# A delta-rule block and a multiplicative FFN: scaling U on ScalarE, head by head, under a new list of steps

## The chip, the cores and the metric

The kernel runs on one core of a Trainium2 chip. The metric is the time of one launch in device microseconds, as the median of the runs. "PE" is TensorE (PEld its weight loads), "DVE" VectorE, "ACT" ScalarE, "POOL" GpSimd and "SP" SyncE, which issues all transfers here.

## The reference

A delta-rule attention over 4 batches x 8 heads x 768 tokens x 48 features, and behind it a feed-forward block whose two branches are multiplied.

```python
k_n = k / (np.linalg.norm(k, axis=-1, keepdims=True) + 1e-06)
for t in range(S):
    y[:, :, t] = np.einsum('bhd,bhde->bhe', q[:, :, t], state)
    v_old = np.einsum('bhde,bhd->bhe', state, kt)
    state = state + bt[:, :, :, None] * np.einsum('bhd,bhe->bhde', kt, vt - v_old)
...
a = x @ w1
b = x @ w2
h = a * b @ w3
return (h @ w_out).astype(np.float32)
```

x is y with the heads side by side: 3072 tokens x 384. The weights come as 64-bit floats and are converted on the chip. w3 and w_out are multiplied into one matrix first (384 wide), and the products of the feed-forward block use a scheme with sums of weights and of tokens that needs fewer products.

## The kernel before

The 768 tokens are cut into 12 chunks of 64. For each chunk:

- **scores** (step name `s`): K K^T and K Q^T for 4 batches x 8 heads. It works in two halves (`r` = 0, 1: two of the four batches each). A half is 48 small products into one pair of PSUM banks (a `ps_w` tile, L433 and L439). One part of it, scaled by beta and the key's norm for each token and head (`wt`), is U (L445, written to `U`). The other is copied to `PT` (L457) and masked (L459). There are two such pairs of banks, taken in turn by all the small products: scores, corner, chain and outputs, and by the inverse, which holds one of them.
- **to_blocks** (`u`), **inverse** (`V`), **corner** (`e`): (1 + U) is inverted for two chunks at once. Blocks of 32 x 32 of U are brought into another layout: for the first two pairs of chunks by copies (L492) and a transpose (L508), for the other four pairs by transfers to DRAM and back (`Ud` L499, `Ub` L510). VectorE then takes 31 steps of two operations (L530/L535 or L541/L546). The result goes back in the same way (L589, or `Vd` L559 and `TT` L571), is transposed (`T`, L599), and two small products (L616) make the block off the diagonal.
- **chain** (`c`): three products (L687) with the state of the chunk before and with the inverse, with VectorE in between (L718, L727, L749). This is the recurrence over chunks. **outputs** (`y`) makes y of the chunk (L786), and ScalarE copies it to `xT` (L805).

Around these stand the loads of k, q, v (`k`, `p`, `v`) and of weights (`P`, converted by ScalarE, VectorE and GpSimd: L837, L840, L842, L844), the fold of w3 and w_out (`t` L880, `f` L895), and the feed-forward block: for the first two chunks plain products (`a`, `b`, L915), for each later pair of chunks products with sums (`m`, L1117, four `ps_f` banks), sums of tokens and of slabs (`G`, `S`, both L200) and the output products (`o`, L1199) with their results (`x`).

Every step is a generator. `ORDER` is a table of 1705 names, written out; each name runs its generator to the next `yield`, and this order holds on every engine. An apostrophe gives a step's elementwise work to the other engine: with it, a sum (L200) goes to VectorE in place of GpSimd, and a copy (L204) to ScalarE or VectorE, whichever it was not.

Of the kernel before, what the change touches and what calls it, by code (L numbers as in the profile page):

```python
# [44 lines left out]
P16 k3 g1 V0 P17 V0 f1 f2 f0 f0 f0 f1 V0 V0 P15 P15 V0 s1 zp t5 P16 f1 P19 P15 V0 zp P17 V0 t6 f2
P18 V0 V0 f2 t6 P16 zp zp P16 p2 V0 P18 g1 t9 V0 P23 v0 t7 P18 f3 V0 g1 P19 t8 V0 t8 t7 P19 P19 f3
t9 P18 t10 V0 d2 V0 P22 P23 t10 P29 d2 zp V0 t11 t11 V0 g1 f4 V0 n0 V0 V0 s0 P23 P23 P20 n0 P22 f5
f4 f5 V0 d2 V0 V0 V0 P22 f3 P29 N1 V0 P21 P21 P20 p3 P22 N1 t14 t15 e0 e0 e0 e0 N0 e0 d2 s2 t14 f5
P20 P20 e0 e0 e0 P25 P25 e1 e1 e1 f4 t12 d3 s2 s2 v1 d3 s2 P29 s2 u2 s2 c0 t12' c0 f7 P24 P24 P29 e1
c0 p3 c0 t15' P25 P21 d3 P26 y0 P28 c1 n1 n1 y0 f6 P26 d3 c1 u2 P21 e1 s3 P24 s3 s3 t13 P26 y0 P27  # L50
e1 s3 e1 f7 t13 s3 s3 P24 u2 e1 f7' u3 P26 u3 c1 P25 s1 u3 V1 V1 V1 b3 P28 b3 P27 b2 b2 c1 N1 p4 V1
V1 V1 V1 V1 y1 y1 P31 P27 P27 P28 V1 V1 V1 b0 f6 V1 V1 V1 V1 V1 V1 f6 P31 b0 c1 c1 b1 P30 P30 P28 b7
b5 c2 V1 V1 d4 b1 y1 a04 a04 b7 a05 a05 b5 a01 a02 a00 P31 P31 P32 P34 a03 P33 V1 V1 V1 V1 a01 a02
P34 a06 b6 v2 V1 V1 a03 a00 n2 P30 P35 d4 a06 P32 V1 b4 P34 V1 V1 V1 P33 P32 P33 p4 a07 P30 n2 P32
V1 V1 V1 V1 V1 V1 b6 b4 b1 c2 b1 P35 a07 P34 b3 P35 e2 b3 P33 zp e2 e2 a03 P35 e2 a02 a01 e2 b7 e3 W
e3 e3 e2 e2 W' k5 k4 d4 a03 d4 b5 W' e2 c2 e3 b7 a02 T c2 g2 g2 a01 p5 v3 a00 g2 g2 g2 g2 g2 y2 c2
y2 d5 d5 b4 a06 T b5 W c2 n3 b4 g2 a00 n3 T e3 T a06 N2 N2 a04 a07 b2 p5 s4 W e3 a04 v4 a07 s4 d5 k6
b2 s4 s4 s4 s4 s4 a05 d5 a05 c3 c3 u4 s5 s5 s5 s5 s5 s5 s5 u5 V2 b0 e3 N2 b6 b0 S0' S0' p6 b6 S0 e3
c3 S0 V2 V2 g3 W W' oA0 W' W' c3 S0 W n4 n4 W S0 s5 xA0 g3 S0' c3 oA0 W S0 c3 V2 V2 y3 oD0 xA0 S0 S0
S0 V2 V2 V2 V2 V2 V2 V2 V2 d6 S0 S0 V2 W S0 oB0 oC0 xA0 s4 V2 V2 V2 xB0 V2 y3 y3 V2 V2 V2 oB0 xB0 V2  # L60
c4 xC0 G1 S0 S0 W V2 V2 xD0 V2 d6 V2 xC0 G1 m10 G1 G1 oC0 G1 G1 m10 m10 m10 m10 m10 m10 xC0 G1 G1 W
W W G1 V2 V2 p6 k7 V2 m10 m10 m10 m10 V2 V2 V2 V2 V2 m10 m10 m10 m10 m10 m10 m10 G1 m10 V2 V2 V2 xC0
xD0 m10 m10 m10 m10 e4 d6 W W W m10 m10 m10 m10 m10 m10 m10 m10 m10 m10 m10 m10' m10 m10 G1 d6 m10
m10 m10 m11 e4 e4 m10 g3 e4 G1 m10 m10 m11 m11 m10 m10 m10 c4 g3 g3 g3 g3 g3 e4 e4 m11 p7 m11 c4 m11
c4 m10' y4 e5 d7 d7 m11 N3 p7 v5 n5 m11 m11 N3 m11 m11 m11 m11 y4 m11 m11 s6 m11 m11 m11 s6 s6 m11
m11 m11 v6 s6 n6 s6 e5 m11 e5 s6 d7 s6 d7 m11 m11 m11 e5 s7 s7 s7 s7 s7 s7 s7 u7 u6 V3 m11 m11 m11
m11 m11 n5 m11 m11 c4 e5 m11 m11 c4 c5 c5 m11 m11 m11 S1 m11 m11 e5 V3 m11 c5 m11 m11 m11 oA1 p8 k8
c5 m11 m11 m11 m11 y5 S1 V3 V3 V3 V3 V3 V3 V3 S1 S1 oD1 S1 S1 xA1 y5 y5 oB1 oA1 xA1 V3 V3 V3 V3 V3
V3 V3 S1 xB1 V3 d8 V3 d8 V3 oB1 xB1 xA1 p8 V3 V3 xD1 oC1 V3 V3 xC1 S1 xC1 G2 m20 G2 G2 G2 G2 G2 G2
G2 G2 m20 m20 m20 V3 xD1 m20 m20 n6 V3 V3 m20 m20 V3 oC1 c5 g4 V3 xC1 V3 V3 V3 V3 V3 V3 m20 m20 m20  # L70
N3 xC1 k9 m20 m20 m20 m20 m20 V3 V3 m20 V3 e6 m20 g4 m20 m20 m20 m20 c5 s6 m20 m20 m20 m20 m20 m20
m20 m20 m20 m20 d8 m20 c6 c6 e6 G2 G2 G2 m20 m20 m20 m20 m20 m20 m20 g4 m20 e6 m21 m20 d8 p9 m20 e6
e6 m20 m21 s8 e7 v7 g4 m21 e6 c6 g4 g4 g4 g4 m20 m20 m20 n7 c6 N4 m21 m21 m21 m21 y6 N4 s8 m21 d9 d9
# [30 lines left out]
def kernel(  # L104
# [311 lines left out]
    def by_parity(x):  # L416
        return x.rearrange("p (a e) t -> p a e t", e=2)
# [978 lines left out]
```

## Time and profile before

| | |
|---|---|
| median of 3 runs | 547.52 us (545.92 to 552.04) |
| the profiled execution | 546.43 us, its span 544.7 us |
| TensorE busy | 511.2 us (94%) |
| weight loads busy | 429.7 us (79%) |
| VectorE busy | 406.1 us (75%) |
| GpSimd busy | 274.8 us (50%) |
| ScalarE busy | 220.3 us (40%) |
| transfers, share of 16 engines | 45.9% on the queue that SP issues |

Shares are of the span and are averages over stages: transfers and conversions of weights fill the first 80 us, the products of the feed-forward block everything from about 100 us on. In a group's row the columns are: line, engine, operation, out<-in, shapes, count | busy us, mean ns of one | idle time of the engine just before, and what ended it. In a row of the timeline: start, length, engine, line, operation, count, and in brackets the idle time before it. In the chain of waits: start, length, what. A matmul of 32-bit data leaves two records, so a step of 32 products has 64.

### The profile page before, as it was taken

What the parts mean: (1) busy time and instruction counts of PE and PEld (TensorE: products, weight loads), DVE (VectorE), ACT (ScalarE), POOL (GpSimd) and SP (SyncE); (2) the same over time, 40 slices, a digit from 0 to 9 for tenths busy, and PEclk for the clock granted to TensorE, in tenths of its full rate; (3) what the DMA queues carried; (4) which work ended last, traced back from release to release, by engine and by line L of the source; (5) the groups of instructions that cost most, each with busy time, mean ns of one, the idle gap of its engine ahead of it and who ended that gap; (6) DMA issues with size and microseconds to landing.
All of it is one profiled execution on the core that took longest, in us unless ns stands there. A gap on an engine that the chain in (4) does not pass through costs nothing.

```text
span 544.7 us, 19913 instructions
## 1 busy us (share of the span) xinstructions
PE 511.2 (94%) x8460; PEld 429.7 (79%) x8460; DVE 406.1 (75%) x882; ACT 220.3 (40%) x452; POOL 274.8 (50%) x295
## 2 busy tenths in 40 slices
PE   3599898999999999999999999999899999999997
PEld 2475565788888987889888789878799888997887
DVE  1789985799778988768987789968688766436553
ACT  3696676847423134432236251343421342412210
POOL 4565664416968994157642487443267301240140
PEclk9999999999999999999999999999999999999999
DMA  8978995668565155644446641654402220020001
GB/s 235 256 194 236 222 163 108 133 147 137 81 104 105 30 126 83 97 90 79 80 93 93 112 88 43 130 84 73 99 19 59 64 51 4 14 76 0 2 0 58
DMA packets 197592, 52.64 MB, mean 97 GB/s; under 512 B 184576, under 2 KB 191872, under 8 KB 197504
## 3 DMA queue, kind: packets, MB, share of 16 engines
q1 hardware_dynamic: 197504, 51.38, 45.9%
q8 instruction: 66, 1.08, 0.8%
q14 instruction: 22, 0.18, 0.1%
HBM read 41.25 MB, written 8.91 MB: 92 GB/s over the span
## 4 chain that ended last, share of the span: by engine, by line
PE 79%; DVE 7%; DMA 5%; ACT 3%; issue 2%; SPq 2%; POOL 1%; DVEq 0%; POOLq 0%; ACTq 0%
PE ps_f L1117 32%; PE ps_f L1199 17%; PE ps_f L915 8%; PE ps_w L687 6%; PE ps_w L786 4%; PE ps_w L616 3%; DMA raw<-in_moe_w_dram 3%; PE ps_f L895 2%; PE ps_w L433 2%; PE ps_w L439 2%; DVE ps_w L535 1%; DVE tb L530 1%; DMA ktok<-in_k_dram 1%; PE ps_f L880 1%; DMA perm<-in_q_dram 1%
## 5 line engine op out<-in xcount | busy, mean ns | idle before, releaser
L200 POOL TENSOR_TENSOR ab<-ab 128x512 f32<-128x512 f32 (+1 forms) x57 | 66.7, 1186 | 65.8 <-DVE ab L1148 33.5
L1199 PE MATMUL ps_f<-w,ab 128*128 128x192 f32 x376 | 65.4, 328 | 0.0
L1117 PE MATMUL ps_f<-xT,w2s 128*128 128x256 f32 x240 | 62.3, 390 | 1.1 <-DVE x_room L1148 0.8
L1117 PE MATMUL ps_f<-xT,w1s 128*128 128x256 f32 x240 | 63.1, 387 | 0.0
L1199 PEld LDWEIGHTS ps_f<-w,ab 128*128 128x128 f32 x376 | 61.8, 191 | 0.9 <-DVE osb L1229 0.2
L1148 DVE TENSOR_TENSOR ab<-ab,ps_f 128x512 f32<-128x512 f32 x70 | 47.4, 680 | 19.2 <-PE ps_f L1117 17.6
L1117 PEld LDWEIGHTS ps_f<-xT,w1s 128*128 128x128 f32 x240 | 43.6, 190 | 10.1 <-issue 1.7
L1117 PEld LDWEIGHTS ps_f<-xT,w2s 128*128 128x128 f32 x240 | 43.7, 190 | 9.8 <-DVE x_room L1148 1.4
L1199 PE MATMUL ps_f<-room,ab 128*128 128x192 f32 x272 | 47.0, 329 | 0.3 <-POOL ab L200 0.2
L546 DVE TENSOR_TENSOR ps_w<-ps_w,tb 128x31 f32<-128x31 f32 (+15 forms) x124 | 43.3, 349 | 4.5
L895 PE MATMUL ps_f<-w2s,w3T 128*128 128x384 f32 x128 | 43.9, 491 | 2.1 <-ACT w3T L204 1.2
L541 DVE TENSOR_TENSOR tb<-ps_w,Ub 128x31 f32<-128x31 f32 (+15 forms) x124 | 41.8, 337 | 4.6 <-DMA Ub<-Ud 1.5
L1199 PEld LDWEIGHTS ps_f<-room,ab 128*128 128x128 f32 x272 | 44.2, 190 | 1.2 <-POOL ab L200 0.5
L805 ACT COPY xT<-ps_w 48x256 f32<-48x256 f32 x96 | 30.5, 365 | 30.4 <-PE ps_w L786 29.8
L1117 PE MATMUL ps_f<-xT,room 128*128 128x256 f32 x160 | 40.3, 384 | 0.0
L673 POOL TENSOR_TENSOR vtok<-vtok,n 128x384 f32<-128x384 f32 x24 | 19.7, 830 | 37.8 <-DMA vtok<-in_v_dram 37.8
L200 POOL TENSOR_TENSOR ab<-ab,x_room 128x512 f32<-128x512 f32 x10 | 12.7, 1274 | 50.0 <-DVE x_room L1148 50.0
L895 PEld LDWEIGHTS ps_f<-w2s,w3T 128*128 128x128 f32 x128 | 23.5, 190 | 17.9 <-POOL w2s L844 1.8
L200 POOL TENSOR_TENSOR xT<-xT 128x256 f32<-128x256 f32 x44 | 32.1, 741 | 7.9 <-DVE xT L200 4.6
L1145 ACT COPY x_room<-ps_f 128x512 f32<-128x512 f32 x20 | 11.7, 585 | 59.4 <-PE ps_f L1117 58.5
L459 POOL TENSOR_TENSOR PT<-PT,smask 128x512 f32<-128x512 f32 x20 | 25.9, 1297 | 17.0 <-ACT PT L457 17.0
L1148 DVE TENSOR_TENSOR x_room<-x_room,ps_f 128x512 f32<-128x512 f32 x40 | 27.3, 682 | 9.1 <-PE ps_f L1117 8.1
(192 smaller groups left out, 1080.6 us busy)
## 6 DMA issues: line engine op xcount, KB each, us to landing
raw<-in_moe_w_dram SPq DMA_DIRECT2D x16, 512.0 KB, 5.5
ktok<-in_k_dram SPq DMA_DIRECT2D x48, 96.0 KB, 3.4
vtok<-in_v_dram SPq DMA_DIRECT2D x24, 192.0 KB, 4.3
raw<-in_moe_w_dram SPq DMA_DIRECT2D x24, 192.0 KB, 4.1
out_dram<-osb SPq DMA_DIRECT2D x46, 96.0 KB, 1.7
raw<-in_moe_w_out_dram SPq DMA_DIRECT2D x8, 384.0 KB, 5.0
perm<-in_k_dram SPq DMA_DIRECT2D x40, 64.0 KB, 3.3
perm<-in_q_dram SPq DMA_DIRECT2D x32, 64.0 KB, 2.8
```

The source lines that it names most:

```text
L200: (dve if other else pool).tensor_tensor(out=out, in0=x, in1=y, op=op)
L459: pool.tensor_tensor(out=PT, in0=PT, in1=smask[:].unsqueeze(1).to_broadcast([P, H, C]), op=ALU.mult)
L541: dve.tensor_tensor(out=tv, in0=V[:, 0 : s + 1, s : s + 1].to_broadcast([P, s + 1, n]), in1=U[:, s, s + 1 : BS].unsqueeze(1).to_broadcast( ...
L546: dve.tensor_tensor(out=o, in0=o, in1=tv, op=ALU.subtract)
L687: pe.matmul(out(ps, r, h, z), lhsT=lhs(r, h, z), rhs=rhs(r, h, z), start=True, stop=True,)
L786: i = pe.matmul(region(h, z, r), lhsT=lhs, rhs=rhs, start=part[n] not in part[:n], stop=part[n] not in part[n + 1 :],)
L805: act.copy(out=xT[f, cc, p:NP:2, b : b + NR, :].rearrange("p a r t -> p r a t"), in_=pyv[f, z, b : b + NR],)
L895: pe.matmul(ps[:, 0:DM], lhsT=w3Ts[jc, kc // 4][:, kc % 4 * P : kc % 4 * P + P], rhs=wo[:, kc], start=(i == 0), stop=(i == KF - 1),)
L915: pe.matmul(ps[:].rearrange("p b c t -> p b (c t)"), lhsT=w[:, m, js], rhs=x[:, c0, m], start=(m == 0), stop=(m == KM - 1),)
L1117: pe.matmul(ps[:, n * g : n * g + n].rearrange("p (b c t) -> p b c t", b=HB, c=2), lhsT=product_weights(i, 2 * r + g), rhs=of[i], start=na ...
L1148: dve.tensor_tensor(out=t, in0=t, in1=cell(what[2]), op=op)
L1199: pe.matmul(ps[b][:, b, :], lhsT=block(u, HF * f + i, z)[:, P * b : P * b + P], rhs=ws_[w][:, i], start=first and i == 0 and (b == 0 or n ...
```

## The change

For the chunks 4 to 11, U of a half is no longer made by one VectorE step over 128x512, but by eight ScalarE operations of 128x64, one for each head, each with that head's column of `wt` as its scale. Chunks 0 to 3 stay as they were. All 1705 steps stand in a new list; each name occurs as often as before, but apostrophes have moved: 18 of the slab sums' steps have one in place of 10, 11 of the token sums' in place of 7, 16 of the `m` steps in place of 13.

```diff
-P11 beta P2 P0 P11 P11 P11 P2 beta P3 k0 K0 P0 beta P0 P0 K0' K0 P6 P6 q0 P2 zd P9 P3 Q0 P2 P6 P3 g0
-g0 g0 k1 P8 Q0' P6 P3 g0 Q0' P9 Q0' K0 P9 g0 g0 g0 P9 zp P8 P10 q1 K0' K1 P13 P10 Q0' s0 P12 P10 P8
...
+P11 beta P2 P0 P11 P11 P11 P2 beta P3 k0 K0 P0 beta P0 P0 K0' K0 P6 P6 P3 K0' q0 P2 zd zd P2 g0 g0
+g0 k1 g0 P6 Q0 g0 P3 g0 P6 K0 P5 P5 P5 Q0 K1 K1 Q0' K1 K1 Q0' P10 P9 P3 P5 P10 q1 P12 g0 g0 P9 Q0 N0
...
-            dve.tensor_tensor(
-                out=by_parity(u[:, r]), in0=psv[:, :, :, 0, :],
-                in1=by_parity(
-                    scale_of(ws, m)[:, r].unsqueeze(2)
-                ).to_broadcast([P, NP, 2, C]),
-                op=ALU.mult,
-            )
-            yield
+            if m < 4:
+                dve.tensor_tensor(
+                    out=by_parity(u[:, r]), in0=psv[:, :, :, 0, :],
+                    in1=by_parity(
+                        scale_of(ws, m)[:, r].unsqueeze(2)
+                    ).to_broadcast([P, NP, 2, C]),
+                    op=ALU.mult,
+                )
+                yield
+            else:
+                for h in range(H):
+                    act.mul(
+                        out=u[:, r, h], in_=psv[:, h // 2, h % 2, 0, :],
+                        mul=scale_of(ws, m)[:, r, h : h + 1],
+                    )
+                yield
```

Lines behind the new code stand 8 higher in the changed kernel (L457 is L465, L616 is L624, and so on); the eight operations are its L456.

The first place is ScalarE's queue in the third round of inverses, chunks 6 and 7. Before (L457 is the PT copy of a score half, L641 and L661 the copies of a corner, L516 the start of an inverse, L1141 and L1145 empty banks of the `m` products):

```order
L457 COPY PT<-ps_w 128x512
L1145 COPY ab<-ps_f 128x512
L457 COPY PT<-ps_w 128x512
L641 COPY T_104<-ps_w 32x2x8x32 x2
L457 COPY PT<-ps_w 128x512 x2
L1145 COPY x_room_97<-ps_f 128x512
L661 ACTIVATE TT_94<-ps_w 32x2x8x32 x2
L516 COPY ps_w<-eye 128x1023
```

and now (L456 is U, L465 the PT copy):

```order
L456 ACTIVATE U_103<-ps_w,wt 128x64 x8
L465 COPY PT<-ps_w 128x512
L1153 COPY ab<-ps_f 128x512
L649 COPY T_104<-ps_w 32x2x8x32 x2
L456 ACTIVATE U_103<-ps_w,wt 128x64 x8
L465 COPY PT<-ps_w 128x512
L456 ACTIVATE U_103<-ps_w,wt 128x64 x16
L465 COPY PT<-ps_w 128x512 x2
L669 ACTIVATE TT_94<-ps_w 32x2x8x32 x2
```

Each PT copy has eight operations ahead of it, and in the third group two halves' U stand ahead of both their PT copies: the second half of chunk 7 and the second half of chunk 6, which comes last in the new list (before, chunk 7's did).

The second place is the same round on VectorE. Before (L445 is U, L390 makes K^T and Q^T of a later chunk, L1148 and L1143 belong to the `m` products, L749, L718 and L727 to the chain):

```order
L445 TENSOR_TENSOR U_103<-ps_w,wt 128x512
L390 STREAM_TRANSPOSE KQ<-perm_95 128x8x64 x2
L1148 TENSOR_TENSOR x_room_97<-x_room_97,ps_f 128x512
L445 TENSOR_TENSOR U_103<-ps_w,wt 128x512 x2
L1148 TENSOR_TENSOR ab<-ab,ps_f 128x512 x3
```

and now (L1156 and L1151 are the former L1148 and L1143, L726 the former L718):

```order
L390 STREAM_TRANSPOSE KQ<-perm_95 128x8x64 x2
L726 TENSOR_TENSOR vtok<-vtok,ps_w 128x768
L1156 TENSOR_TENSOR ab<-ab,ps_f 128x512
L1156 TENSOR_TENSOR x_room_97<-x_room_97,ps_f 128x512
L329 TENSOR_REDUCE ss<-sq 128x8
L1156 TENSOR_TENSOR ab<-ab,ps_f 128x512 x3
L200 TENSOR_TENSOR ab<-ab 128x512
L1151 TENSOR_TENSOR ab<-ps_f,ab 128x512
L200 TENSOR_TENSOR ab<-ab 128x512
```

The U steps are gone, and sums of slabs (L200) that GpSimd made stand among the `m` steps.

The third place is ScalarE's queue at the start, ahead of the first inverse. Before (L492 copies blocks of U, L837 and L840 convert a piece of weights):

```order
L492 COPY xT_79<-U_103 32x32x16
L492 COPY xT_79<-U_103 96x32x16
L837 ACTIVATE w2s<-raw 128x384
L840 ACTIVATE raw<-raw 128x384
L492 COPY xT_79<-U_103 32x32x16
L516 COPY ps_w<-eye 128x1023
```

and now (L500 is the former L492, L524 the former L516):

```order
L465 COPY PT<-ps_w 128x512
L500 COPY xT_79<-U_103 96x32x16
L500 COPY xT_79<-U_103 32x32x16
L524 COPY ps_w<-eye 128x1023
L529 COPY ps_w<-eye 128x1
```

The conversion that stood between the last two copies of U has moved away.

More of the change, by code (lines that the diff above doesn't have):

```diff
@@ L45 @@
[L45 to L49, printed above, removed]
@@ new lines @@
+k10 y7 oD2 S2 S2 S2 S2 oB2 V4 m21 V4 V4 V4 V4 V4 V4 V4 V4 xA2 xB2 V4 V4 V4 V4 d10 V4 d10 V4 oC2 S2
+oA2 S2 oB2 xA2 xB2 xC2 c7 xA2 xC2 xD2 S2 G3 G3 G3 m30 V4 V4 V4 V4 V4 oC2 xC2 s8 G3 G3 G3 G3 G3' V4
+V4 p10 m30 m30 m30 m30 m30 m30 m30 m30 m30 m30 m30 V4 G3 G3 n8 G3 G3 m30 m30 m30 V4 V4 V4 m30 m30
+m30 V4 m30 m30 m30 m30 m30 m30 m30 m30 m30 m30 m30 V4 V4 k11 v9 xD2 n9 n8 g5 c7 n9 m30 m30 m30 m30
+c8 xC2 V4 e8 c8 d10 e8 m30 m30 m30 m30 m30 m30 m30 m30 e8 m31 g5 e8 m30 g5 g5 m30 d10 e8 e9 m31 g5
+g5 m30 m30' m30 p11 m31 e8 m31 m31 g5 g5 c8 c8 m30' N5 m31 m31 m31 m31 m31 y8 c8 N5 d11 d11 e9 m31
@@ new lines @@
+m31 c8 p11 m31 m31 m31 m31 m31 y8 e9 e9 s10 s10 s10 m31 m31 m31 s10 s10 m31 m31 d11 c9 s10 s10 c9
+d11 m31 m31 s11 s11 s11 s11 s9 s11 m31 m31 m31 m31 m31 s11 u10 u11 V5 m31 m31' m31 e9 s11 m31 m31
+m31 m31 m31' m31 m31 v11 e9 c9 m31 m31 m31 m31 m31 m31 S3' c9 oA3 xA3 m31 s11 S3 S3 S3 y9 V5 N5 m31
+V5 V5 V5 V5 V5 V5 V5 oD3 v10 S3 n10 oB3 y9 oA3 V5 V5 V5 V5 V5 V5 V5 xB3 S3 S3 S3 xA3 oC3 oB3 y9 V5
+V5 V5 G4 G4' xA3 V5 c9 m40 xB3 xC3 G4 xD3 xC3 n10 G4' G4 G4 G4 G4 G4 G4 V5 V5 V5 oC3 c9 xC3 V5 V5
+m40 m40 m40 m40 m40 m40 m40 m40 m40 n11 G4 m40 m40 m40 m40 m40 V5 V5 V5 V5 V5 c10 m40 m40 m40 m40 V5
@@ L100 @@
+S5' S5 S5' S5 S5' o5 x5 x5 x5 o5 x5 x5 x5 x5 x5 x5 o5 x5 x5 x5 x5
 """
```

98 lines of the change are left out of this document (45 added, 53 removed).

## The prediction

> **What bounds the kernel now.** I read the page first, then the stretches of the span, then the chain and the groups of instructions.
>
> ```profile
> span 544.7 us, 19913 instructions
> PE 511.2 (94%) x8460; PEld 429.7 (79%) x8460; DVE 406.1 (75%) x882; ACT 220.3 (40%) x452; POOL 274.8 (50%) x295
> PEclk9999999999999999999999999999999999999999
> PE 79%; DVE 7%; DMA 5%; ACT 3%; issue 2%; SPq 2%; POOL 1%; DVEq 0%; POOLq 0%; ACTq 0%
> ```
>
> TensorE is busy for 94% of the span and carries 79% of the chain that ended last. The same by stages (columns: stretch, its length, busy time of PE, PEld, DVE, ACT and POOL):
>
> ```profile
> 0.00:28.00 28.00, 12.34 (x313) 10.86 (x316) 13.32 (x34) 14.47 (x27) 14.56 (x26) 1.00 0.96 247
> 28.00:76.00 48.00, 44.31 (x310) 28.14 (x302) 43.13 (x115) 35.84 (x65) 30.03 (x34) 1.00 0.84 205
> 102.00:137.00 35.00, 34.88 (x398) 29.12 (x395) 32.51 (x82) 22.53 (x50) 14.52 (x14) 1.00 0.76 144
> 232.00:284.00 52.00, 51.59 (x750) 45.14 (x753) 43.52 (x98) 14.23 (x32) 33.08 (x34) 1.00 0.44 89
> 439.00:520.00 81.00, 80.75 (x1067) 70.18 (x1056) 43.39 (x66) 25.18 (x52) 18.28 (x17) 1.00 0.08 21
> ```
>
> The reader is to see two kernels here. In the first 28 us TensorE is idle more than half of the time, behind loads (DMA share 0.96). From about 100 us on it hardly stops: 34.88 of 35, 51.59 of 52, 80.75 of 81 us. There a faster VectorE buys nothing by itself; only TensorE's waits can be gained, and they are few. What can be lost is larger: any producer that comes later than TensorE's queue expects it adds its whole delay. So I price the change by the places where TensorE has least room.
>
> **What the change removes and adds.** The rows are VectorE's step, ScalarE's nearest operations, and the slab and token sums, which have one line on both engines:
>
> ```profile
> L445 DVE TENSOR_TENSOR U<-ps_w,wt 128x512 f32<-128x512 f32 x24 | 16.5, 687 | 10.8 <-PE ps_w L439 10.7
> L457 ACT COPY PT<-ps_w 128x512 f32<-128x512 f32 x20 | 11.7, 586 | 30.8 <-DVE U L445 30.8
> L521 ACT COPY ps_w<-eye 128x1 f32<-128x1 f32 x6 | 1.0, 163 | 0.2
> L805 ACT COPY xT<-ps_w 48x256 f32<-48x256 f32 x96 | 30.5, 365 | 30.4 <-PE ps_w L786 29.8
> L200 DVE TENSOR_TENSOR ab<-ab 128x512 f32<-128x512 f32 x16 | 14.2, 901 | 5.9 <-POOL ab L200 3.9 <-PE ps_f L1199 1.7
> L200 POOL TENSOR_TENSOR ab<-ab 128x512 f32<-128x512 f32 x44 | 56.5, 1297 | 63.4 <-DVE ab L1148 33.5 <-PE ps_f L1199 17.1 <-DVE ab L200 11.7
> L200 DVE TENSOR_TENSOR xT<-xT 128x256 f32<-128x256 f32 x6 | 3.1, 520 | 0.0
> L200 POOL TENSOR_TENSOR xT<-xT 128x256 f32<-128x256 f32 x44 | 32.1, 741 | 7.9 <-DVE xT L200 4.6 <-DMA xT<-xT 2.5
> ```
>
> VectorE loses 16 of its 24 U steps: 16 x 0.687 = 11.0 us. But the new list also sends 11 more 512-wide sums and 3 more 256-wide ones to VectorE instead of GpSimd (36 and 13 where 25 and 10 were), and one 512-wide copy fewer: 11 x 0.90 + 3 x 0.52 - 0.68 = +10.8 us. VectorE's total stays; GpSimd is the one relieved, by 11 x 1.3 + 3 x 0.74, some 16 us, of which I count nothing, since half of its span is idle.
>
> ScalarE gets 128 operations, eight for each half of a chunk, 128x64 with a scale for each partition. No row has one. Bounds: not under the 163 ns of one element, not over the 365 ns of 256 elements in a row of eight. Between 163 ns (1 element) and 586 ns (512) a straight line gives 0.215 us for 64; I take that: 1.72 us a half in place of 0.69, 27.5 us in all, on an engine that is 60% idle. In total they are covered. They count where something waits for that very half.
>
> The Trainium skill, ScalarE: Activation LUTs, section "What ACT_TABLE_LOAD costs", says that an activation takes 186 ns plus 0.833 ns an element, that each per-partition pointer operand adds about 93 ns, and that neighbours overlap by about 93 ns. The 586 ns row lies 27 ns below its 613. By it a half would be 8 x 0.239 + 0.09 = 2.0 us (an estimate), and the sum below would be 0.5 us higher. The same page's "Rules for kernel authors" would leave multiplications to VectorE; the trace agrees only for the half as a whole (0.69 against eight operations).
>
> **Bank release.** A score half lies in one of the two ps_w pairs of banks, and its pair comes free after U and the PT copy. Before, the PT copy waited for VectorE's U (30.8 us in the row of L457), so it took 0.69 + 0.59 = 1.28 us; now 1.72 + 0.59 = 2.31 us, on one engine. TensorE's rows for one step of each kind:
>
> ```profile
> 486.85 16.96 PE ps_f L1117 x76
> 187.19 1.08 PE ps_w L687 x64
> 117.41 19.62 PE ps_f L915 x90
> L433 PE MATMUL ps_w<-KQ 48*64 48x128 f32 x384 | 26.9, 281 | 0.8 <-ACT PT L457 0.4 <-DVE vtok L718 0.4
> ```
>
> 76 records are 19 L1117 products, 0.89 us each; 64 are one L687 product; 90 are 15 L915 products of 1.31 us; a score half is 26.9/24 = 1.12 us. In the new list the least room between a half and the next writer of its pair is two L1117 products and another half, 2 x 0.89 + 1.12 = 2.9 us, at four places (the first half of chunk 7, the second of chunk 8, both of chunk 10); elsewhere 3.3 to 5.9. 2.9 covers 2.31 unless ScalarE is late. I put +0.5 us there (0 to 7; the upper end at 0.365 us an operation, when a half holds its pair 3.5 us and two neighbouring halves 7.0).
>
> **The third round of inverses.** This is the tight place. U of chunks 6 and 7 goes to DRAM and back (Ud, Ub), is inverted in 31 steps on VectorE, goes out and back again (Vd, TT), is transposed (T) and enters the corner product L616:
>
> ```profile
> 232.36 0.69 DVE L445 TENSOR_TENSOR U<-ps_w,wt 128x512 f32<-128x512 f32 x1 [0.74 <-PE ps_w L439]
> 233.07 5.07 SPq L499 DMA_DIRECT2D Ud<-U  x8
> 241.53 0.34 SPq L510 DMA_DIRECT2D Ub<-Ud  x1
> 245.85 0.19 DVE L541 TENSOR_TENSOR tb<-ps_w,Ub 128x31 f32<-128x31 f32 x1 [1.51 <-DMA Ub<-Ud]
> 278.95 1.93 SPq L571 DMA_DIRECT2D TT<-Vd  x4
> 282.27 0.71 DVE L599 STREAM_TRANSPOSE T<-TT 128x512 f32<-128x512 f32 x1 [0.34 <-DMA TT<-Vd]
> 282.79 1.10 PE L1117 MATMUL ps_f<-xT,w1s 128*128 128x256 f32 x4
> 283.82 0.76 PE L616 MATMUL ps_w<-T,U 33*33 33x32 f32 x64
> ```
>
> Each link starts as the one before ends; VectorE even idles 1.51 us for Ub. From the end of the last score half (232.3) T is ready after 50.7 us, and TensorE gets there after 51.5: room 0.8 us. In between TensorE had 26 L1117 products, 7 of L1199, 5 of L687, one L616 step and one L786. The new list has 25, 7, 3, 1 and 1: 0.89 + 2 x 1.08 = 3.05 us less, so it arrives after 48.5 us. The chain does not get shorter: ScalarE's queue holds U of chunk 7's first half, its PT copy, then 16 activations for that chunk's second half and chunk 6's. The first half ends 1.12 + 2 x 0.89 + 1.12 = 4.0 us before the last one, so by 0.215 us U of chunk 7 is done at -4.0 + 0.1 + 1.72 + 0.59 + 1.72 = +0.1 to +0.5 us, against +0.75 for VectorE's before; I let the chain gain 0.2 and be 50.5. TensorE then waits 50.5 - 48.5 = **2.0 us** (1.0 at 0.163 us an operation, 4.1 at 0.365). What is late next is all of TensorE's queue behind that corner, and nothing later gives it back, as 439 to 520 us shows.
>
> In the other rounds the U chain also lengthens, by 2 to 3 us after the last half, but there the list puts more work in: before the corner of chunk 4 four L915 products and one L687 product more and one L1117 product less (+5.4 us), for chunk 8 two L687 more and one L1117 less (+1.3), for chunk 10 seven L1117 more and one L687 less (+5.1). I count nothing.
>
> **The start.** Loads and conversions come in another order; U is still VectorE's there.
>
> ```profile
> 37.75 1.09 ACT xT L492
> 38.84 0.45 ACT w2s L837
> 39.29 0.45 ACT raw L840
> 39.76 1.09 ACT xT L492
> 71.36 0.69 ACT w L837
> 73.73 1.98 ACT TT L589 x2
> 76.57 0.73 PE ps_w L616 x48
> L508 DVE STREAM_TRANSPOSE Ub<-xT x2: 1245/1246/1246, 41.1 to 101.8; 128x1024 f32<-128x1024 f32 x2
> 137.04 0.69 PE ps_w L616 x50
> ```
>
> The weight conversion between the copies of U (0.9 us) is moved behind them, and the piece whose load ended at 71.36 is asked for earlier. The first inverse can start some 2 us earlier and the second (101.8) 2 to 4. But TensorE must have the same folds done before the corner at 76.57, so I give that corner 1 us; and before the corner of chunk 2 (137.04) the list has four L915 products less and one L687 and one small one more, 3.5 us less work, while the second inverse still needs about 33 of its 35.2 us from 101.8. What comes early there waits. Net 0, bounds -4 (all kept) and +2 (nothing gained, the corner waited for).
>
> **Sum.** The profiled execution took 546.43 us. +2.0 +0.5 +0 = 548.9. The median of the three runs is 547.52, 1.1 above that execution, so the forecast for the median is 547.5 + 2.5 = **550.0 us**, own range 545 to 553.
>
> **Rivals.** *A, slower: ScalarE holds the banks.* It decides at 2.9 - 0.59 = 2.3 us a half, 0.29 us an operation. Beyond it, each late half is a TensorE wait, because the halves stand in pairs. For it: no row bounds a scaled operation below 0.29, and ScalarE also empties ps_f. Against: the line through its rows says 0.215. At 0.365 us it costs 7 + 4.1 = 11 us (559), at 0.30 about 4; taken at 556. By the skill's 2.0 us a half it would just not begin. *B, faster: the earlier start is kept.* If the corners of chunks 2 and 6 find TensorE with enough work after all, the 4 us stay, and with them about 2 us of the clock's dip,
>
> ```profile
> 390.00:394.00 4.00, 2.52 (x68) 1.80 (x62) 1.21 (x3) 1.30 (x3) 0.00 (x0) 0.89 0.39 131
> ```
>
> where TensorE worked 2.52 of 4 us at a granted 0.89 and which need not recur: 547.5 - 6 = 541.5. Against it: the step counts above. *C: it doesn't do what it says.* VectorE is not relieved, the third round has room that I don't see, and the list is as good as the old one: 547.5.
>
> **How the numbers follow.** Forecast 0.42, C 0.15, A 0.27, B 0.16. A change of 1% (5.5 us) is about what a measurement of this kernel can tell from none: below 542.0 is faster, above 553.0 slower. Forecast and C are both within, 0.57; A gives slower 0.27, B faster 0.16. The range 541.5 to 559 reaches from B's time to A's upper end and leaves out what lies beyond either.
>
> **What would show it.** Right: 128 activations of 0.2 to 0.25 us, 16 groups; VectorE's busy time within 4 us of 406, GpSimd's near 258, ScalarE's near 248; at the first corner product of chunk 6 a TensorE wait of 1 to 4 us, released by VectorE's T; the first L508 near 39 us, the corner of chunk 2 within 2 us of 137. Wrong: no wait at that corner (then the round has room, B or C); activations over 0.29 us, or score halves and products that wait for PT copies all over (A); a corner of chunk 2 near 133 us with no wait ahead of it (B); or a loss in the last 100 us, where I count none.

## The result and the profile after

The changed kernel takes 552.93 us (median of 20 runs, 547.73 to 558.46) against 548.41 us (545.92 to 552.04, 20 runs) for the kernel before. The ratio is 1.0066, with a 95% interval of 1.0041 to 1.0091: slower by some 3.6 us. The ratio leaves out three slow runs of the changed kernel, which the median of all 20 holds, so the medians lie 4.5 us apart. The forecast was +2.5 us, a change of less than 1%; that holds. The forecast median of 550.0 us is 2.9 us short, of which 0.9 is the kernel before itself, whose median of 20 runs is above that of the three. How the sum was made up does not hold, as the sections below show.

The profiled execution took 551.95 us, 5.5 more than that of before. The lines that answer those shown of before (first the page's span, busy time, granted clock and chain, then the stretches with PE, PEld, DVE, ACT and POOL, at the same bounds):

```profile
span 550.2 us, 20037 instructions
PE 511.3 (93%) x8460; PEld 428.5 (78%) x8460; DVE 404.6 (74%) x879; ACT 246.6 (45%) x581; POOL 260.6 (47%) x281
PEclk9999999999999999999999999999999999999999
PE 30%; DVE 12%; DMA 7%; SPq 5%; issue 2%; ACT 1%; DVEq 0%
```

```profile
28.00:76.00 48.00, 43.79 (x364) 28.51 (x368) 44.36 (x118) 35.81 (x66) 31.97 (x37) 1.00 0.87 206
102.00:137.00 35.00, 33.54 (x503) 26.96 (x502) 28.94 (x70) 20.99 (x49) 14.21 (x15) 1.00 0.85 140
232.00:284.00 52.00, 51.55 (x682) 45.37 (x682) 43.38 (x100) 18.57 (x53) 27.68 (x28) 1.00 0.42 84
439.00:520.00 81.00, 79.77 (x1100) 68.65 (x1099) 46.55 (x68) 25.61 (x53) 15.05 (x14) 1.00 0.12 28
```

TensorE is busy for 511.3 us, as before (511.2). So the whole 5.5 us is time in which TensorE is idle: 38.9 us in place of 33.5 (span less busy time). The 30% of TensorE in the chain that ended last can't be set beside the 79% of before: the shares of the changed kernel add up to 57%, those of before to 99%, because its chain is followed back only to 232 us (in a second profile of the changed kernel, which experiment 5 took, TensorE has 46 of 57). The idle time by stage, for two profiles of the changed kernel (span less PE busy of each stretch):

| stretch, us | before | changed | changed, second profile |
|---|---|---|---|
| 0 to 28 | 15.7 | 15.4 | 16.2 |
| 28 to 102 | 7.3 | 7.5 | 7.6 |
| 102 to 180 | 1.2 | 3.0 | 3.6 |
| 180 to 284 | 1.1 | 1.5 | 0.9 |
| 284 to 400 | 3.3 | 5.3 | 2.8 |
| 400 to the end | 4.9 | 6.2 | 5.9 |

Against this one profile of before, two stages lose in both: 102 to 180 us (about 2 us) and the time behind 400 us (about 1). For the first of them the 1.2 us of before is not a fixed figure: the kernel of experiment 3 (the old list, with U of chunks 4 and 5 on VectorE) runs the same instructions in the same order as the kernel before up to 224 us, and its profile has 2.6 us there. Only 0.4 to 1.0 us of the loss stand clear of that. The inverse of chunks 6 and 7 (the third round of the prediction, 232 to 284 us), on which the forecast put its largest term, lost nothing up to its corner at 285 us. TensorE's larger waits behind 102 us in the first profile of the changed kernel (columns: who waited <- for what: sum in us, times, longest):

```profile
PE ps_f L923 <- ACT ab L935: 0.7, 1, 0.7
PE ps_f L923 <- POOL w2s L852: 0.7, 2, 0.5
PE ps_f L923 <- DVE ab L939: 0.5, 1, 0.5
PE ps_w L433 <- DVE KQ L390: 3.0, 2, 2.1
PE ps_f L1207 <- DVE osb L1237: 1.0, 1, 1.0
PE ps_w L624 <- issue: 0.5, 1, 0.5
PE ps_w L624 <- DVE T L607: 0.9, 2, 0.7
PE ps_f L1125 <- DVE x_room L1156: 0.8, 1, 0.8
PE ps_f L1207 <- DVE ab L200: 0.8, 1, 0.8
```

The row for `x_room` stands in the profile of before too, with the same 0.8 us. None of the rows is a wait for U or for a PT copy; of those for T, which the inverse makes from U, the longest is 0.65 us at chunk 8's corner (365.6 us), and it is not in the second profile. The largest is for K^T and Q^T (L390) of a later chunk, at 231.7 us (0.88) and 311 us (2.09). In the second profile it is 1.8 us in two waits (longest 1.2), the products L923 wait 2.5 us, the 0.8 us for VectorE's sum (L200) stands there too, and the 1.0 us for L1237 is gone.

The operations themselves (groups by shape, then one half in the timeline):

```profile
L456 ACT ACTIVATE U<-ps_w,wt 128x64 f32<-128x64 f32 x128 | 28.2, 349 | 18.5 <-PE ps_w L439 15.8 <-DMA perm<-in_k_dram 2.5
L465 ACT COPY PT<-ps_w 128x512 f32<-128x512 f32 x20 | 12.6, 638 | 0.5 <-DVE U L446 0.5
```

```profile
226.38 1.74 ACT L456 ACTIVATE U<-ps_w,wt 128x64 f32<-128x64 f32 x8 [1.18 <-PE ps_w L439]
```

One record lasts 349 ns, but 128 of them cover only 28.2 us, 0.22 us each: neighbours overlap. Eight take 1.74 us. A mean of one record, read as the price of one, would have given 2.8 us a half.

### The profile page after: what moved, and what is told of

The parts are those of the page before. It is cut to its first block, busy times and chain, and to the rows that moved or that the text cites. A ratio compares the mean times of both kernels' runs of the same rounds, so it can differ in the third digit from the quotient of the medians.

```text
span 550.2 us, 20037 instructions
## 1 busy us (share of the span) xinstructions
PE 511.3 (93%) x8460; PEld 428.5 (78%) x8460; DVE 404.6 (74%) x879; ACT 246.6 (45%) x581; POOL 260.6 (47%) x281
## 4 chain that ended last, share of the span: by engine, by line
PE 30%; DVE 12%; DMA 7%; SPq 5%; issue 2%; ACT 1%; DVEq 0%
PE ps_f L1125 15%; PE ps_f L1207 9%; DVE tb L549 3%; DVE ps_w L554 3%; SPq L297 3%; PE ps_w L695 2%; DMA perm<-in_q_dram 1%; DVE KQ L390 1%; DMA TT<-Vd 1%; DMA perm<-in_k_dram 1%; PE ps_w L794 1%; DMA Ud<-U 1%; PE ps_w L624 1%; DVE ab L200 1%; DMA Vd<-Ub 1%
## 5 line engine op out<-in xcount | busy, mean ns | idle before, releaser
L200 POOL TENSOR_TENSOR ab<-ab 128x512 f32<-128x512 f32 (+1 forms) x48 | 53.7, 1132 | 72.0 <-DVE ab L1156 30.0
L1156 DVE TENSOR_TENSOR ab<-ab,ps_f 128x512 f32<-128x512 f32 x70 | 47.7, 683 | 25.7 <-PE ps_f L1125 23.4
L1125 PE MATMUL ps_f<-xT,w1s 128*128 128x256 f32 x240 | 63.8, 389 | 0.3 <-ACT ps_f L1137 0.2
L1125 PE MATMUL ps_f<-xT,w2s 128*128 128x256 f32 x240 | 61.1, 386 | 0.8 <-DVE x_room L1156 0.8
L1125 PEld LDWEIGHTS ps_f<-xT,w1s 128*128 128x128 f32 x240 | 43.4, 189 | 10.9 <-ACT x_room L1153 2.2
L1125 PEld LDWEIGHTS ps_f<-xT,w2s 128*128 128x128 f32 x240 | 44.0, 190 | 8.0 <-DVE x_room L1156 1.2
L200 POOL TENSOR_TENSOR xT<-xT 128x256 f32<-128x256 f32 x41 | 30.2, 749 | 33.0 <-DVE xT L200 23.0
L813 ACT COPY xT<-ps_w 48x256 f32<-48x256 f32 x96 | 30.5, 366 | 31.2 <-PE ps_w L794 30.5
L1125 PE MATMUL ps_f<-xT,room 128*128 128x256 f32 x160 | 40.2, 384 | 0.0
L390 DVE STREAM_TRANSPOSE KQ<-perm 128x512 f32<-128x512 f32 x36 | 24.5, 698 | 17.6 <-DMA perm<-in_k_dram 4.7
L456 ACT ACTIVATE U<-ps_w,wt 128x64 f32<-128x64 f32 x128 | 28.2, 349 | 18.5 <-PE ps_w L439 15.8
L1156 DVE TENSOR_TENSOR x_room<-x_room,ps_f 128x512 f32<-128x512 f32 x40 | 27.3, 681 | 12.4 <-PE ps_f L1125 10.0
L433 PE MATMUL ps_w<-KQ 48*64 48x128 f32 x384 | 29.4, 284 | 7.1 <-DVE KQ L390 3.4
```

Source lines behind the costliest of these rows:

```text
L200: (dve if other else pool).tensor_tensor(out=out, in0=x, in1=y, op=op)
L390: dve.transpose(out=KQ[:, bs, :, i, :].rearrange("p b a t -> p (b a) t"), in_=src[:, bs].rearrange("p b a x d -> p (b a) (x d)"),)
L433: pe.matmul(ps[half(z), 0, n : n + 128], lhsT=x[:, 0, :], rhs=x.rearrange("p j t -> p (j t)"), start=True, stop=True,)
L456: act.mul(out=u[:, r, h], in_=psv[:, h // 2, h % 2, 0, :], mul=scale_of(ws, m)[:, r, h : h + 1],)
L813: act.copy(out=xT[f, cc, p:NP:2, b : b + NR, :].rearrange("p a r t -> p r a t"), in_=pyv[f, z, b : b + NR],)
L1125: pe.matmul(ps[:, n * g : n * g + n].rearrange("p (b c t) -> p b c t", b=HB, c=2), lhsT=product_weights(i, 2 * r + g), rhs=of[i], start=na ...
```

## Experiments

All kernels of one group ran on the same chip beside the kernel before; two groups, and so two numbers from different experiments, need not share a chip. Ratios are to the kernel before, with a 95% interval. Theory L was that the new list makes the loss, theory U that the eight operations make it.

**1. One half of the change at a time.** The new list, with U of all chunks on VectorE (against the changed kernel; the step ahead of the `else` then stands for every chunk):

```diff
             if m < 4:
                 dve.tensor_tensor(
...
-            else:
-                for h in range(H):
-                    act.mul(
...
```

> The new list with U made by VectorE for all twelve chunks, as before. Theory L (the list makes the loss: TensorE's waits of 2.09 us at 311 us and 0.88 us at 231.7 us for K^T and Q^T whose loads stand later in SP's queue, of 0.97 and 0.75 us behind VectorE's moved sums, some 2 us around 110 to 145 us; the eight operations cost nothing): as long as the changed kernel or longer, 1.004 to 1.010 of the kernel before, the wait at 311 us within 1 us of 2.09, VectorE busy about 416 us. Theory U (the eight operations make it, by holding banks and delaying the inverse): 0.998 to 1.003.

Measured: 1.0136 (1.0092 to 1.0180). And the old list with U of chunks 4 to 11 on ScalarE (against the changed kernel):

```diff
-P11 beta P2 P0 P11 P11 P11 P2 beta P3 k0 K0 P0 beta P0 P0 K0' K0 P6 P6 P3 K0' q0 P2 zd zd P2 g0 g0
+P11 beta P2 P0 P11 P11 P11 P2 beta P3 k0 K0 P0 beta P0 P0 K0' K0 P6 P6 q0 P2 zd P9 P3 Q0 P2 P6 P3 g0
...
```

> The old list with U of chunks 4 to 11 made by the eight ScalarE operations. Theory L: 0.998 to 1.003 of the kernel before; score halves end their bank use 1 us later and nothing waits for more than 1 us in sum. Theory U: 1.005 or more, waits of TensorE for PT copies ahead of the score halves that stand close together (310, 383 us) and 1 to 2 us at the first corner product of chunk 6, where the old list leaves 0.8 us.

Measured: 1.0135 (1.0091 to 1.0180). Both theories fall. Either half alone costs 1.35% in these runs, about 7 us, and both together cost half of that: each part makes good something of the other. The waits tell a part of what that is. The old list with U on ScalarE, TensorE's waits from 102 to 400 us:

```profile
PE ps_f L1125 <- ACT ab L1149: 1.7, 1, 1.7
PE ps_f L1125 <- DVE room L1237: 1.6, 1, 1.6
PE ps_f L1125 <- ACT x_room L1153: 1.6, 2, 1.0
PE ps_w L695 <- ACT TT L669: 1.2, 2, 0.9
PE ps_w L433 <- ACT PT L465: 1.0, 1, 1.0
```

5.5 of these 7.1 us end with ScalarE. The timeline around the first of them, VectorE's last step of chunk 8's weights (`wt`) and then ScalarE's queue:

```profile
298.93 0.19 DVE L370 TENSOR_TENSOR wt<-wt,nt 128x32 f32<-128x32 f32 x1
299.20 1.75 ACT L456 ACTIVATE U<-ps_w,wt 128x64 f32<-128x64 f32 x8 [4.38 <-PE ps_w L794]
300.79 0.65 ACT L1149 ACTIVATE ab<-ps_f 128x512 f32<-128x512 f32 x1
301.27 0.65 ACT L1153 COPY x_room<-ps_f 128x512 f32<-128x512 f32 x1
301.74 0.68 ACT L1149 ACTIVATE ab<-ps_f 128x512 f32<-128x512 f32 x1
```

ScalarE sat idle for 4.38 us ahead of U, and three empties of ps_f banks stood behind it; TensorE's m product waited 1.7 us for the first. The bracket names outputs of TensorE (L794) that U does not read. Of what it reads, the half was done at 293.7 us and the weights at 299.1, so the weights were late; that is read from the times, no row says it here (one does in experiment 5). On VectorE, U stood behind its own weights in the same queue, and these empties were in another.

The new list with U on VectorE shows the opposite case. VectorE near 311 us in a second profile of that kernel (its run is number 7), then TensorE's wait there:

```profile
310.28 1.30 DVE L390 STREAM_TRANSPOSE KQ<-perm 128x512 f32<-128x512 f32 x2 [3.71 <-DMA perm<-in_q_dram]
311.51 0.91 DVE L749 TENSOR_TENSOR S<-S,ps_w 112x768 f32<-112x768 f32 x1
312.35 0.67 DVE L445 TENSOR_TENSOR U<-ps_w,wt 128x512 f32<-128x512 f32 x1
```

```profile
PE ps_w L433 <- ACT PT L457: 4.0, 1, 4.0
```

Here the list puts U of chunk 8's second half behind transposes of chunk 9, which wait 3.71 us for a load of q. On VectorE U and with it the PT copy are late, the half keeps its banks, and TensorE waits 4.0 us (1.9 in the first profile). On ScalarE U passes that queue: in the changed kernel it ran at 306.1 us, and what is left there is the wait for K^T and Q^T itself, 1.2 to 2.1 us. So this place shows how the operations help the new list, but not all that they are worth: the first profile of the new list with U on VectorE has no more idle time of TensorE than the changed kernel's (39.1 and 38.9 us), though its runs were longer.

**2. Is it ScalarE's queue?** In the old list with U on ScalarE, U is moved behind the empties at two places; nothing else changes its place on TensorE, VectorE, GpSimd or SP. ScalarE's queue at the first:

```diff
-L456 ACTIVATE U_103<-ps_w,wt 128x64 x8
-L1149 ACTIVATE ab<-ps_f 128x512
-L1153 COPY x_room_97<-ps_f 128x512
-L1149 ACTIVATE ab<-ps_f 128x512
+L1149 ACTIVATE ab<-ps_f 128x512
+L1153 COPY x_room_97<-ps_f 128x512
+L1149 ACTIVATE ab<-ps_f 128x512
+L456 ACTIVATE U_103<-ps_w,wt 128x64 x8
```

> The old list with U on ScalarE, and U moved in ScalarE's queue alone at two places: for the first half of chunk 8 behind three empties of the feed-forward banks, for the second half of chunk 11 behind one. Theory Q (a U that waits for its weight or its half holds the queue, and the empties behind it hold TensorE's banks): the waits of 1.70 us at 301.5 and 1.04 us at 397.6 us ahead of L1125 go, TensorE's idle time falls by 2 to 3 us and the ratio from 1.0135 to 1.008 to 1.010. Theory B (a half holds its own pair of banks too long): both waits stay or turn into waits ahead of score halves, ratio 1.012 to 1.015.

Measured: 1.0074 (1.0034 to 1.0115). TensorE's idle time falls from 40.8 to 38.1 us, and among the waits behind 102 us no row of L1125 names ScalarE any more. Theory Q holds for these two places as far as the waits go. What they were worth in time is less sure: the two ratios come from two groups on two chips and their intervals overlap, and of the 3 us between them the split in experiment 7 gives 1.2 to the waits and the rest to the clock. The two rows of chunks 4 and 5 (163.9 and 170.5 us) stay:

```profile
PE ps_w L695 <- ACT TT L669: 1.2, 2, 0.9
PE ps_w L433 <- ACT PT L465: 0.9, 1, 0.9
```

**3. The halves that stand close together.** On top of 2, chunks 4 and 5 go back to VectorE:

```diff
-            if m < 4:
+            if m < 6:
```

> The old list with the two moves in ScalarE's queue, and U of chunks 4 and 5 on VectorE again (eight operations only from chunk 6 on). If the pair of halves that stand close together in that round holds the banks (0.94 us ahead of L433 at 163.9, 0.86 us ahead of L695 at 170.5 us, both released by ScalarE): both waits go, TensorE's idle time falls by 1.5 to 2 us and the ratio from 1.0074 to 1.002 to 1.005. If the rest of the loss is spread over all rounds: 1.006 to 1.009.

Both waits went, as expected: from 150 to 175 us waits of 0.4 and 0.2 us are left, neither for ScalarE, and the idle time is 35.8 us in place of 38.1. But the ratio is 1.0090 (1.0052 to 1.0129), which is what I expected for a loss that is spread over all rounds. The intervals of 2 and 3 overlap, so the runs do not show that the time followed. That ScalarE held the banks there is shown by the profile; what it was worth in time is not.

**4. More time on ScalarE.** In the changed kernel the first four of the eight operations are issued twice, then all of them:

```diff
-                for h in range(H):
+                for h in [0, 1, 2, 3] + list(range(H)):
```

> The changed kernel with the first four of the eight operations of each half issued twice: 12 operations, 2.6 us a half in place of 1.74. By the forecast's limit (from 2.3 us a half on, something waits) it passes the limit by 0.3 us at four places and lengthens the chain of the third round by 0.9 to 1.8 us: 1 to 3 us over the changed kernel, 1.008 to 1.012 of the kernel before. By a straight line through the run with all operations twice (4.5 us a half, 36 us over the changed kernel, so 13 us for each us a half): 11 us over the changed kernel, 1.025 to 1.028.

A half took 2.56 us. Measured: 1.0155 (1.0120 to 1.0191), 5 us over the changed kernel, above the limit's 1 to 3 and half of the straight line's 11.

```diff
-                for h in range(H):
+                for h in [h for h in range(H) for _ in range(2)]:
```

> The changed kernel with every one of the 128 operations issued twice, so ScalarE's time for a half goes from 1.74 to about 3.5 us. By the forecast's table of room (2.9 us from a half to the next writer of its banks at four places, 3.3 to 5.9 elsewhere) a half that holds its banks 4.1 us costs 1.2 us at four places, some 2 us at the next ones, and 2 to 3.5 us at the corner of chunk 6: 6 to 10 us over the changed kernel, 1.017 to 1.025 of the kernel before, with waits ahead of score halves and products released by PT copies. If ScalarE's place in the chain has more room than that: under 1.012.

A half took 4.53 us, not 3.5: a head's second operation starts 0.34 us behind its first, where the next head's first follows 0.21 us behind (medians of the trace). With 12 operations, in which three other heads stand between the two, all follow 0.20 us apart. Measured: 1.0723 (1.0685 to 1.0761), 587.8 us. I had expected 6 to 10 us over the changed kernel, and it is some 35. Two things add up, waits and clock (TensorE's waits, then four stretches):

```profile
PE ps_w L624 <- ACT PT L465: 10.3, 4, 5.4
PE ps_w L695 <- ACT PT L465: 7.9, 3, 3.9
PE ps_w L433 <- ACT PT L465: 6.1, 5, 2.5
```

```profile
255.33:258.74 3.41, 0.00 (x0) 0.00 (x0) 0.26 (x1) 3.22 (x13) 0.00 (x0) 1.00 0.36 59
258.75:265.58 6.83, 6.53 (x80) 4.92 (x80) 0.69 (x1) 4.01 (x8) 0.00 (x0) 0.50 0.59 135
330.42:333.83 3.41, 1.07 (x5) 0.59 (x4) 1.61 (x3) 3.25 (x12) 0.00 (x0) 1.00 0.00 0
333.84:340.66 6.82, 6.71 (x103) 6.02 (x104) 0.69 (x1) 4.42 (x18) 0.00 (x0) 0.50 0.25 42
```

These waits for PT copies make 24.3 us, and not only ahead of score halves: corner (L624) and chain products (L695) take the same banks in turn. And after each long wait TensorE ran at half of its clock for 3.4 or 6.8 us (third number from the end: 0.50). The mean granted clock of these runs is 0.971; 2.9% of a span of 586 us is 17 us lost at most.

**5. The wait for K^T and Q^T.** In the changed kernel, chunk 9's loads of k go ahead of chunk 7's returns in SP's queue, and the transposes that hold their buffer go forward with them. SP's queue:

```diff
-L579 DMA TT_94<-Vd 32x16x32 x4
-L586 DMA T_106<-Vd 32x8x32 x4
 L297 DMA perm_95<-in_k_dram 32x16x32 x2
...
+L579 DMA TT_94<-Vd 32x16x32 x4
+L586 DMA T_106<-Vd 32x8x32 x4
```

> The changed kernel with the loads of chunk 9's k and q earlier: k's ahead of the returns of chunk 7's inverse in SP's queue, the four transposes that hold their buffer moved forward with them. Theory L: the wait of 2.09 us ahead of the score half at 311 us falls under 0.5 us and the time by 1 to 2 us against the changed kernel (ratio to before 1.002 to 1.005). Theory U, or a reserve elsewhere: the wait goes, but comes back at the corner of chunk 8 (then longer than its 0.65 us at 365.6 by 1 us or more), ratio 1.0055 to 1.008.

Measured: 1.0105 (1.0073 to 1.0138): longer, against both. The wait at 311 us was gone, but another of 4.1 us stood ahead of chunk 7's corner (VectorE's timeline, then the waits from 304 to 309 us):

```profile
300.22 1.30 DVE L390 STREAM_TRANSPOSE KQ<-perm 128x512 f32<-128x512 f32 x2 [4.45 <-PE ps_w L794]
```

```profile
ACT U L456 <- DVE wt L370: 8.0, 1, 8.0
PE ps_w L624 <- ACT PT L465: 4.1, 1, 4.1
```

Chunk 9's K^T takes the buffer that the outputs of chunk 6 (L794) still read. Moved forward, its transposes held VectorE for 4.45 us; chunk 8's weights came late, ScalarE's U waited 8.0 us for them, the PT copy stood behind U, and the corner product behind the PT copy. I had moved the step past a buffer that I had not followed. With the outputs and the weights moved as well (TensorE's queue):

```diff
-L433 MATMUL ps_w<-KQ 64x128 x2
...
 L794 MATMUL ps_w<-KQ,S 48x64 x16
 L794 MATMUL ps_w<-PT,X 48x64 x32
 L794 MATMUL ps_w<-KQ,S 48x64 x16
+L433 MATMUL ps_w<-KQ 64x128 x2
```

> The changed kernel with chunk 9's loads earlier, this time with what holds them moved too: the outputs of chunk 6 (they read the buffer that chunk 9's K^T takes) ahead of the first half of chunk 8, the weights of chunk 8 ahead of the transposes of chunk 9. If the list's order of loads makes the wait of 2.09 us: it falls under 0.6 us, no new wait of over 1 us appears at the second corner product of chunk 7, and the time is 1.5 to 2.5 us under the changed kernel. If the round has no slack at all: the wait goes and comes back at the corner of chunk 8 (0.65 us now), no gain.

Measured: 1.0051 (1.0022 to 1.0080), the changed kernel beside it 1.0056 (1.0017 to 1.0094). No gain that the runs can show. Its one profile is of its longest run (558.7 us): the wait at 311 us is gone in it and one of 1.6 us stands ahead of a corner product (L624) at 309.7 us, for a copy of the outputs that were moved (L813). As a single long run it is no more than a sign, and where the wait went stays open.

The changed kernel itself, in the same group:

> The changed kernel once more, beside the other three on one chip: 1.004 to 1.009 of the kernel before. If the waits of its first profile are the program's own, the ones at 311 (2.09 us, score half for K^T and Q^T), 344.7 (0.97) and 475.2 us (0.75) stand at the same places within 0.3 us; if they are chance, elsewhere.

Of the three waits, those at 311 us (1.24 us in place of 2.09, a larger difference than the 0.3 us expected) and 475 us (0.75, at 470.7) came again; that at 344.7 us did not, so it does not belong to every execution.

**6. The sums.** In the changed kernel every sum's apostrophe is as at its place in the old list. That gives 20 sums back to GpSimd, and puts eight on VectorE. VectorE at one of these eight:

```diff
 L554 TENSOR_TENSOR ps_w<-ps_w,tb 128x10x22
+L200 TENSOR_TENSOR ab<-ab 128x256
 L549 TENSOR_TENSOR tb<-ps_w,Ub 128x231
```

> The changed kernel with the apostrophes of the slab and token sums as in the old list, so that GpSimd makes them again: VectorE's busy time falls by some 8 to 10 us to about 396, GpSimd's rises by 11 to 15 us. If VectorE's sums make the waits of 0.97 us (344.7) and 0.75 us (475.2): both go, 1 to 2 us under the changed kernel. If they were moved because GpSimd is late with them: new waits for sums that GpSimd makes (1.27 us each in place of 0.68 to 0.9), as long as the changed kernel or up to 5 us longer.

Measured: 1.0186 (1.0140 to 1.0232). VectorE's busy time fell to 395.4 us and GpSimd's rose to 272.2; the two waits went. But one of 5.0 us came, put down to GpSimd (the waits from 102 to 400 us, then GpSimd's timeline):

```profile
PE ps_f L1207 <- POOL ab L200: 5.0, 1, 5.0
```

```profile
180.87 1.59 POOL L200 TENSOR_TENSOR ab<-ab 128x256 f32<-128x256 f32 x2 [5.02 <-DVE ab L200]
```

The releaser's own row speaks against reading it so: GpSimd had sat idle for 5.02 us for a sum on VectorE, one of the eight, which stands between two steps of an inverse. So the 20 alone:

```diff
-L200 TENSOR_TENSOR ab<-ab 128x512
 L1151 TENSOR_TENSOR ab<-ps_f,ab 128x512
 L200 TENSOR_TENSOR ab<-ab 128x512
```

> The changed kernel with 20 slab and token sums given back from VectorE to GpSimd, and none the other way (the kernel before this one also put eight sums on VectorE; its wait of 5.0 us ended with a sum of GpSimd that had itself waited for one of those on VectorE). If GpSimd makes sums too late for this list: waits of L1207 for sums of GpSimd and 1.010 to 1.020 of the kernel before. If the loss came from the eight sums put on VectorE: 1.003 to 1.008, as the changed kernel, with VectorE near 385 us, GpSimd near 288, and no wait for GpSimd's sums over 1 us.

Measured: 1.0030 (0.9994 to 1.0066). VectorE's busy time is 394.0 us (I had said 385), GpSimd's 279.4, no wait for a sum on GpSimd is in the profile, the waits at 344.7 and 475 us are gone, and behind 400 us TensorE is idle for 5.1 us (6.2 and 5.9 in the changed kernel). The moved sums bring nothing to the new list that the runs show. They cost it, if anything, about 1 us: the interval holds 1.0, and it overlaps that of the changed kernel.

**7. The new list with U on VectorE again.**

> The new list with U on VectorE once more, since its profile shows no more idle time of TensorE (39.1 us) than the changed kernel's (38.9) while its runs were some 4 us longer. If the operations are worth that in the new list: 1.010 to 1.016 of the kernel before again, and its profile shows waits that the changed kernel's two profiles don't have. If the first six runs were chance: 1.003 to 1.008.

Measured: 1.0252 (1.0211 to 1.0293); its profile shows the 4.0 us above. That the same kernel is at 1.0136 in one group and at 1.0252 in another goes with the clock: span times granted clock (means over the compared runs) is 550.6 and 551.1 us, but the rest of the span, the most that the clock can have taken, is 3.5 and 7.8 us. Why the clock was lower in all six runs of the second group is not shown. Split in this way, all kernels:

| kernel | span x clock, us | lost to the clock at most, us |
|---|---|---|
| before, in four groups | 543.9, 544.4, 543.3, 543.9 | 2.1, 1.9, 1.6, 1.7 |
| changed (20 runs; again) | 547.5; 546.9 | 2.9; 2.1 |
| new list, U on VectorE (two groups) | 550.6; 551.1 | 3.5; 7.8 |
| old list, U on ScalarE | 549.8 | 3.7 |
| the same, U behind empties | 548.6 | 1.9 |
| the same, chunks 4, 5 on VectorE | 546.9 | 2.6 |
| changed, 20 sums to GpSimd, eight to VectorE | 549.0 | 7.6 |
| changed, 20 sums to GpSimd alone | 546.1 | 1.4 |
| changed, loads earlier (first; second) | 548.3; 547.9 | 3.8; 2.3 |
| changed, 12 operations; 16 operations | 552.4; 569.3 | 1.9; 16.9 |

None beats the kernel before. The nearest, the changed kernel with 20 sums given back, is not told from it.

## Why the prediction was right, and where it was not

- **What bounds it.** Right: TensorE's work stayed 511 us, and in the profiles the loss is waits of TensorE.
- **The operations.** Right: 28.2 us in all (27.5 estimated), 1.74 us a half (1.72). What I wrote would show it, records of 0.2 to 0.25 us, was wrong: a record lasts 0.35 us and they overlap. By my own sign (over 0.29 us is A) that record would have spoken for A. The Trainium skill, ScalarE: Activation LUTs, "What ACT_TABLE_LOAD costs", has 332 ns for one by its parts (an estimate), and the trace agrees with its median of 340 ns; the 93 ns of overlap are too few, (1.74 - 0.34)/7 = 0.20 us from one to the next here, where the page gave 0.239.
- **Busy times.** Right: VectorE 404.6 (406 +- 4), GpSimd 260.6 (258), ScalarE 246.6 (248).
- **"GpSimd is the one relieved, ... of which I count nothing".** Right: giving the sums back changes the time by no more than the runs resolve. What I did not count is the other side, VectorE's queue with those sums in it: 0.75 us at 475 us.
- **Bank release, +0.5.** The term was 0, inside its 0 to 7: in the new list no wait for a PT copy shows. Rival A's mechanism is real, in the old list (1.0 us at L433) and with longer operations. Its limit of 2.3 us a half lies between 1.74, where no such wait shows, and 2.56, where they make 2.7 us; no run places it closer, and the loss there is more than the 1 to 3 us that I expected.
- **The third round, +2.0.** Failed in size and in cause. TensorE came to chunk 6's corner 48.1 us after the last score half (48.5 forecast; from 237.25 to 285.34), but T was ready after 47.2 us, not 50.5:

```profile
277.44 0.33 SPq L567 DMA_DIRECT2D Vd<-Ub  x1
280.07 1.92 SPq L579 DMA_DIRECT2D TT<-Vd  x4
282.04 3.43 SPq L586 DMA_DIRECT2D T<-Vd  x4
283.74 0.67 DVE L607 STREAM_TRANSPOSE T<-TT 128x512 f32<-128x512 f32 x1
285.34 0.47 PE L624 MATMUL ps_w<-T,U 33*33 33x32 f32 x32
286.35 0.46 PE L624 MATMUL ps_w<-T,U 33*33 33x32 f32 x32 [0.54 <-issue]
```

  The step that failed is "The chain does not get shorter", with its gain of 0.2 us. From the last score half to the inverse's first step it took 12.2 us against 13.5, and from Vd's issue to TT's 2.63 us against 4.63. It is the list and not chance: T was ready 49.9 to 50.7 us after the last half in all four profiles of the old list, wherever U was made, and 46.6 to 48.2 in all nine of the new list with at most 12 operations a half, 46.6 with U on VectorE. The first step is earlier in each of the nine (11.2 to 12.9 us, against 13.5 to 14.0); the way from Vd to TT is not a property of the list, for the old list has 2.6 to 4.6. What in the list brings the first step forward was not followed. The wait that is left, 0.54 us, stands inside the corner product and does not end with VectorE's T. The profile names no releaser; the `T<-Vd` issues that ended at 285.5 are the nearest, but that is argued, not shown.
- **The start, 0.** First inverse at 39.4 us (39 forecast), second at 97.7 in place of 101.8: right. Corner of chunk 2: I said within 2 us of 137; it came at 133.25 after a wait of 0.44 us, so the earlier start reached TensorE. It was not kept: the products L923 waited at 114, 130, 139 and 145 us, 1.9 us in all (2.5 in the second profile), for weights and emptied banks that I had not looked for, and 102 to 180 us lost about 2 against the one profile of before, where these products waited for nothing. In the profile of experiment 3, with the same program in that stage as before, they waited 1.7 us. So the term should have been between +0.4 and +2, and no run tests it.
- **What was missed.** SP's queue: the list puts chunk 9's loads behind chunk 7's returns (issued at 291.9 in place of 285.3), and q's load waits for k's transposes in the one buffer. That is 1.2 to 2.1 us at 311 us. I had compared TensorE's, ScalarE's and VectorE's order in that round and not SP's. Behind 400 us I counted nothing, and TensorE lost about 1 us there (5.9 and 6.2 us of idle time; 4.9 to 5.4 in the four profiles of the old list).
- **Rival C** ("the list is as good as the old one") was put as a list by itself. The list by itself costs 1.35%: it is a list for U on ScalarE.

So +2.5 was met by luck: the largest term of the sum was wrong, and others were missing, 1 to 2 us for the late loads, about 1 behind 400 us and 0.4 to 2 at the start. Which of them make up the 3.6 us of the runs is read from the waits of two profiles; no run took one of them away alone and was told from the changed kernel.

## What to carry to other kernels

When work moves to another engine, ask what it now waits for in that engine's queue and what stands behind it there: U waits for its weights and its half wherever it runs, but on ScalarE the empties of TensorE's banks stood behind that wait. In an order that was made as a whole, the parts of a change are not a sum: here each half alone cost 7 us and both 3.6. Compare the order on every engine that issues, loads included, follow each buffer that a moved step needs, and follow a wait's releaser to what it waited for itself before it gets the blame.

## What the runs showed of the hardware

The clock takes part in the price of a wait. A step of 32 chain products that takes 1.08 us took 1.96 us at half clock (394.17 us in the trace of the kernel before). In every trace here the stretches at half clock lie on a grid of 3.413 us (in the run with all operations twice they begin at 170.00, 241.68, 258.75, 333.84 us: all differences are whole multiples). I laid that grid over all fourteen traces, from 28 us on, and took TensorE's idle time of each window at full clock: of 14 windows with 1.71 us or more, half of a window, all 14 were followed by half clock; of 46 with 1.1 to 1.7 us, 8; of some 2,000 with less, one, with 1.10 us. A window at half clock costs up to half of its 3.4 us, 1.7 us (an estimate from its length). The grid lies otherwise in each execution, so a wait of 1.5 us can fall into one window in some and over two in others; by the same estimate it then costs 1.5 us in one execution and up to 3.2 in another. The Trainium skill, TensorE: Matmul & The Clock Gate, "What's actually happening", states the free-running window of 3,413 ns and the half clock, and the traces agree; its section "Why this matters for your kernels" asks for no gaps over about 3 us, and here less was enough: 1.48 us of idle time in the window that ended at 393.1 us, in the kernel before.
